# Two bit operations of a weight conversion write to PSUM instead of SBUF, and come behind another piece of a step

## The chip, the cores and the metric

The kernel runs on one core of a Trainium2 chip. The metric is the time of one execution on the device in microseconds (us); the kernel before takes 1632.99 us (median of three runs).

A core has five engines that run side by side, each with its own queue of instructions, worked in order: TensorE (PE in the profile) multiplies matrices and transposes; VectorE (DVE) and ScalarE (ACT) work element by element; GpSimd (POOL) does so too; SyncE (SP) issues the transfers (DMA) from and to device memory. Data lie in SBUF; PE writes its products to PSUM, [...]from which DVE and ACT fetch them. An instruction that needs another engine's result, or a buffer that another engine still reads, waits on a semaphore, and everything behind it in the same queue waits too.

## The reference

Attention with a threshold, a Fourier mix over sequence and model dimension, and a layer-normed channel product with a residual (8 batches, 8 heads, 576 tokens, head size 64, so a model width of 512; the hidden width is 2048):

```python
scores = (1.0 / np.sqrt(64)) * np.matmul(q, k.transpose(0, 1, 3, 2))
thresh = np.max(scores, axis=-1, keepdims=True) - tau
scores = np.where(scores >= thresh, scores, -1e9)
attn = np.exp(scores - np.max(scores, axis=-1, keepdims=True))
attn = attn / (np.sum(attn, axis=-1, keepdims=True) + 1e-09)
x = heads_side_by_side(np.matmul(attn, v))            # (8, 576, 512)

u = x + np.real(np.fft.fft(np.fft.fft(x, axis=1), axis=2))
un = (u - mean(u)) / np.sqrt(var(u) + 1e-06)           # over the 512
out = u + np.maximum(un @ w_ch1, 0.0) @ w_ch2          # 512 -> 2048 -> 512
```

The two weight matrices `w_ch1` and `w_ch2` arrive as 64-bit floats. The engines compute in 32-bit floats, so the kernel converts the weights on the chip, from the bit patterns: this is the part that the change touches.

## The kernel before

**Steps.** The attention is cut into 160 steps: 8 batches, 4 pairs of heads, 5 query tiles. `step(i)` does the 20 steps of the first batch, `second_batch(i)` those of the second, a loop at the end the others. In a step, `scores(i)` multiplies queries by keys on PE (L431, for the last tile L437) into the PSUM tile `sc`; `softmax(i)` takes the row maximum on DVE (L455), the exponential on ACT (L463), and the threshold and the sum on DVE (L471). `transposed_weights(i - 1)` transposes the weights of the step before on PE, in the PSUM tiles `pe` (L534, L537) and `pw` (L552), from which ACT copies them to SBUF (`ends` L540 and L544, `e_t` L554 and L556). `weighted_values` multiplies them by the values on PE (`pv`, L581); DVE or ACT fetches the result (L587, L589).

**Filling.** From the second batch on, PE also has the Fourier mix of the batch before (`mixing`: tiles `py` L684, `pa` L701; POOL folds at L614 and adds at L727) and the channel product of ready tokens (`channels`: `rows.load` transposes to `pn`, L774, which ACT copies at L779 and L780; `hidden` makes `ph`, L814, which ACT (L819) and DVE (L821) read in turn). `fill()` puts some of it into a step, three times a step.

**Order.** Over the first two batches everything is in `manual_schedule`: the order of the instructions on every engine is the order in which the Python code emits them. From the third batch on (L1394) that holds for PE alone, the others being ordered by a scheduler.

**PSUM.** Two double banks have the tag `sc`. The other four banks have the tag `mm`, and all other tiles share them: `pd` (products that fill PE, L112), `pm` (column means, L361), `pr` (mirrored rows, L371), and `pe`, `pw`, `pv`, `py`, `pa`, `pn`, `ph`, `po`. A new tile takes over the bank of an earlier one, and the first instruction that writes to it waits for the last one that read the earlier tile.

**Conversion.** `convert` (L280) is a generator; each `next` emits one stage of one chunk of 128 x 512 weights. There are 32 chunks, 16 of `w_ch1` in the first batch (one for each of the steps 0 to 15) and 16 of `w_ch2` in the second, in the order of `PLAN` (L1268), with two chunks in some steps. The stages:

1. SP's DMA brings 512 KB of raw pairs of 32-bit words (L287) into a stretch of `hs`, or where room is (`w`, `stage`).
2. DVE takes the top 20 bits of the mantissa (L297) to the destination in `w1` or `w2` (`w` in the profile), and the 11 bits of the exponent (L300) to `power`, which lies in `hs` or `u_t`.
3. ACT turns the mantissa into a float from 1 to 2 (L305) and the exponent into the bit pattern of a power of two (L308).
4. DVE adds the low word's part of the mantissa (L312).
5. POOL multiplies by the power (L317).
6. ACT takes the sign (L319), POOL multiplies by it (L320).

In the first batch stages 4 to 6 of a chunk are emitted in the next step's softmax. Then, in the chunk's own step, come

```python
if i in chunks:
    next(chunks[i])            # stage 2
if i > 0:
    transposed_weights(i - 1)
if i in chunks:
    next(chunks[i])            # stage 3
```

In `second_batch` stages 2 and 3 come side by side, by two calls of `advance(first)`, behind `transposed_weights`. Where a step has two chunks, `advance` emits stage 2 of both and then stage 3 of both. After the conversion of four chunks of `w_ch1` that make up 512 columns, PE forms the columns' means, and DVE and POOL subtract them (`less_mean`, L377).

Of the kernel before, what the change touches and what calls it, by code (L numbers as in the profile page):

```python
# [10 lines left out]
INT32 = mybir.dt.int32  # L11
UINT32 = mybir.dt.uint32
ALU = mybir.AluOpType
ACT = mybir.ActivationFunctionType
# [33 lines left out]
def kernel(  # L48
# [25 lines left out]
    WC = 512  # L74
# [10 lines left out]
    ps = ctx.enter_context(tc.tile_pool(name="ps", bufs=2, space=bass.MemoryType.PSUM))  # L85
# [19 lines left out]
    def busy(n):  # L105

        for _ in range(n):
            pd = ps.tile([128, 4, 128], FP32, tag="mm", bufs=4, name="pd")
            four = bass.AP(
                tensor=ones.tensor, offset=ones.offset, ap=[list(ones.ap[0]), [0, 4], [1, 128]]  # L110
            )
            nc.tensor.matmul(pd[:, :, :], ones[:, :], four, start=True, stop=True)  # L112
# [31 lines left out]
    def load_v(n):  # L144

        b, p = n // NPAIR, PAIRS[n % NPAIR]
        vt = v_in[n % 2]
        for j in range(2):
            h = 2 * p + (j + p) % 2
            nc.sync.dma_start(  # L150
                out=vt[:, j:8:2, :], in_=v[b, h, 0:512, :].rearrange("(t p) d -> p t d", p=128)
            )
            nc.sync.dma_start(out=vt[64 * j : 64 * j + 64, 8 + j, :], in_=v[b, h, 512:576, :])
# [12 lines left out]
    for u in range(2):  # L166
# [14 lines left out]
        out=q_scale[:], in0=tau_t[:], scalar1=0.0, scalar2=SCALE, op0=ALU.is_ge, op1=ALU.mult  # L181
# [3 lines left out]
        out=below[:], in0=tau_t[:], scalar1=0.0, scalar2=-3.0e38, op0=ALU.is_lt, op1=ALU.mult  # L185
# [3 lines left out]
        out=tau_pos[:], in0=tau_t[:], scalar1=0.0, scalar2=-1.0, op0=ALU.max, op1=ALU.mult  # L189
# [87 lines left out]
    shift = const.tile([128, 1], FP32, name="shift")  # L277
    nc.vector.memset(shift[:], -float((1023 - 127) << 23))

    def convert(src, dst, raw, power):  # L280

        if src.dtype == FP32:
            nc.sync.dma_start(out=dst, in_=src)
            return
        nc.sync.dma_start(out=raw, in_=src.bitcast(INT32).rearrange("p (c n) -> p c n", c=2))  # L287
        pairs = raw.rearrange("p c (n two) -> p c n two", two=2)
        low, high = pairs[:, :, :, 0], pairs[:, :, :, 1]
        dst = dst.rearrange("p (c n) -> p c n", c=2)  # L290
        bits = dst.bitcast(INT32)
        power = power.rearrange("p (c n) -> p c n", c=2)
        sign = high.bitcast(FP32)

        yield

        nc.vector.tensor_scalar(  # L297
            out=bits, in0=high, scalar1=0xFFFFF, scalar2=None, op0=ALU.bitwise_and
        )
        nc.vector.tensor_scalar(  # L300
            out=power, in0=high, scalar1=20, scalar2=0x7FF,
            op0=ALU.logical_shift_right, op1=ALU.bitwise_and,
        )
        yield
        nc.scalar.activation(out=dst, in_=bits, func=ACT.Copy, bias=1.0, scale=2.0**-20)  # L305


        nc.scalar.activation(  # L308
            out=power, in_=power, func=ACT.Relu, bias=shift[:, :], scale=float(1 << 23)
        )  # L310
        yield
        nc.vector.scalar_tensor_tensor(  # L312
            out=dst, in0=low.bitcast(UINT32), scalar=2.0**-52, in1=dst,
            op0=ALU.mult, op1=ALU.add,
        )
        yield
        nc.gpsimd.tensor_tensor(out=dst, in0=dst, in1=power.bitcast(FP32), op=ALU.mult)  # L317
        yield
        nc.scalar.activation(out=sign, in_=high, func=ACT.Sign)  # L319
        nc.gpsimd.tensor_tensor(out=dst, in0=dst, in1=sign, op=ALU.mult)  # L320
# [100 lines left out]
    def scores(i):  # L421
        n, t = divmod(i, NT)
        qT, kT = heads[n][0:2]

        nh = 2 if t < 4 else 1
        sc = [ps.tile([128, 2, 512], FP32, tag="sc", name=f"sc{j}") for j in range(nh)]
        if t < 4:
            for c in range(2):
                for j in range(2):
                    hp, k0 = slice(64 * j, 64 * j + 64), D * (1 - j)  # L430
                    nc.tensor.matmul(  # L431
                        sc[j][:, c, 0:HALF], qT[hp, 128 * t : 128 * t + 128],
                        kT[hp, k0 + HALF * c : k0 + HALF * (c + 1)], start=True, stop=True,
                    )
        else:
            for c in range(2):
                nc.tensor.matmul(  # L437
                    sc[0][:, c, 0:HALF], q_ends[:, :], kT[:, D + HALF * c : D + HALF * (c + 1)],
                    start=True, stop=True,
                )  # L440
        steps[i] = (sc, nh)
# [735 lines left out]
    def step(i):  # L1177

        n, t = divmod(i, NT)
        scores(i)  # L1180

        def stages(count):
            for _ in range(count if i - 1 in chunks else 0):
                next(chunks[i - 1], None)

        def next_stages():
            stages(2)

        def last_stage():
            stages(1)  # L1190
            chunks.pop(i - 1, None)

        if t == 1 and n > 0:
            softmax(i, lambda: weighted_values(n - 1, 1), next_stages, last_stage)
            load_v(n + 1)
        elif t == 3:
            softmax(i, lambda: weighted_values(n, 0), next_stages, last_stage)
        else:
            softmax(i, None, next_stages, last_stage)
        if t == 1 and n > 0:  # L1200
            pass
        elif later and later[0][0] <= i:
            later.pop(0)[1](i)
        else:
            busy(2 if i < NCHUNK else 1)
        if t == 2:
            scale_q(n + 1)
        if t == 3:
            prep_pair(n + 1)
        if t == 1:  # L1210
            prep_ends(n)
        if i in chunks:
            next(chunks[i])
        if i > 0:
            transposed_weights(i - 1)
        if i in chunks:
            next(chunks[i])
        while after and after[0][0] <= i:
            after.pop(0)[1]()
        if i > 0 and i + 3 < NCHUNK:  # L1220
            chunks[i + 3] = w1_chunk(i + 3)
        if t == 2 and n > 0:
            folds.append(fold_rows(n - 1))
        if folds and next(folds[0], True):
            folds.pop(0)
# [26 lines left out]
    chunks = {0: w1_chunk(0)}  # L1252
# [27 lines left out]
    chunks = {}  # L1280

    def advance(at):
        for run in chunks.get(at, ()):
            next(run, None)

    def transfers(first):
# [32 lines left out]
    def second_batch(i):  # L1319

        nonlocal budget
        n, t = divmod(i, NT)
        first = i - per_batch
        if first != 1:
            scores(i)
        if first == 0:

            transposed_weights(i - 1)
        softmax(
            i, None, lambda: (advance(first - 1), advance(first - 1)), lambda: advance(first - 1)  # L1330
        )
        chunks.pop(first - 1, None)
        transfers(first)
        fold_more()
        if first == 0:
            weighted_values(n - 1, 1)
            scores(i + 1)
            column_means(LAST)
            copy_mean(LAST)
            folds.append(fold_rows(n - 1))  # L1340
            while folds:
                fold_more()
            load_v(n + 1)
            start_batch(0)
            mix(3)
            mix(3)
        elif first == 1:
            mix(3)
            transposed_weights(i - 1)
            mix(2)  # L1350
            mirrored(LAST)
            for c, eng in ((1, nc.vector), (3, nc.vector), (0, nc.gpsimd), (2, nc.gpsimd)):
                less_mean(eng, LAST, c)
            advance(first)
            advance(first)
        elif first == 2:
            mix(2)
            transposed_weights(i - 1)
            mix(2)
            weighted_values(n, 0)  # L1360
            advance(first)
            advance(first)
        else:
            fill()
            transposed_weights(i - 1)
            advance(first)
            advance(first)
            fill()
            if t == 3:
                prep_pair(n + 1)  # L1370
            fill()
            if t == 2:
                weighted_values(n, 0)
            if t == 0:
                weighted_values(n - 1, 1)
                folds.append(fold_rows(n - 1))
                load_v(n + 1)
        if t == 1:
            prep_ends(n)
        if t == 2:  # L1380
            scale_q(n + 1)
        if first == 16:
            fold_halves(1)
        if first < 3:
            budget += 3 * per_slot
# [95 lines left out]
```

## Time and profile before

| | |
|---|---|
| runs | 1632.99, 1632.99, 1630.95 us |
| span of the profiled execution | 1631.3 us |
| busy, share of the span | PE 97%, DVE 72%, ACT 50%, POOL 40% |
| busy, 0 to 115 us | PE 103.17, DVE 101.61, ACT 79.03, POOL 87.31 us |
| busy, 115 to 265 us (150 us) | PE 136.19, DVE 123.00, ACT 93.75, POOL 86.71 us |
| busy, 265 to 1631 us (1366 us) | PE 1344.41, DVE 948.79, ACT 644.99, POOL 485.25 us |

"Busy" is the time in which an engine was executing, in one profiled execution. The chain that ended last is followed back from the last instruction, at each step to what released it; it tells which engine set the time. A row of a tile or a line gives the number of instructions with the least, median and greatest duration in ns. A row of the timeline gives start, duration, engine, line, operation, the tile written and the tiles read, the shapes, the count, and in brackets the idle time before it with what ended it. The granted PE clock is 1.00 at full speed.

### The profile page before, as it was taken

The numbers are of one execution on the slowest core, as the hardware profiler recorded it, in microseconds if no ns is written. First come the engines' busy times: TensorE is split into PE (matmuls) and PEld (weight loads), VectorE is DVE, ScalarE is ACT, GpSimd is POOL, SyncE is SP. The second block draws the span as 40 slices with busy tenths as digits, with TensorE's granted clock in tenths as the row PEclk, the third lists the DMA queues.
The fourth block names the chain that finished last, engine by engine and source line by source line (L and its number), as shares of the span: only waits on it lengthen the run. The fifth ranks groups of instructions, "written<-read, shape, count | busy, mean of one in ns | idle before, by whom it ended". The sixth has DMA issues, their size and how long they took to land.

```text
span 1631.3 us, 27898 instructions
## 1 busy us (share of the span) xinstructions
PE 1583.8 (97%) x10346; PEld 1248.7 (77%) x10346; DVE 1173.4 (72%) x2518; ACT 817.8 (50%) x1738; POOL 659.3 (40%) x875
## 2 busy tenths in 40 slices
PE   8998999999999999999999999999999999999998
PEld 4555655577887888878888778877878788889998
DVE  7997886667758686857576868786787869664445
ACT  5765665544455454645445546454636455523111
POOL 6784673042421452244342244224352344124332
PEclk9999999999999999999999999999999999999999
DMA  6423222101110101110011010111111110000000
GB/s 162 123 56 113 74 75 57 40 17 22 20 38 17 34 9 43 23 29 16 21 23 36 17 34 11 41 23 35 17 27 32 22 29 2 14 7 7 14 14 14
DMA packets 203084, 57.41 MB, mean 35 GB/s; under 512 B 193827, under 2 KB 193829, under 8 KB 202950
## 3 DMA queue, kind: packets, MB, share of 16 engines
q1 hardware_dynamic: 200438, 55.34, 14.5%
q8 instruction: 82, 1.34, 0.4%
q10 hardware_dynamic: 2512, 0.30, 0.1%
q14 instruction: 52, 0.43, 0.1%
HBM read 46.02 MB, written 9.44 MB: 34 GB/s over the span
## 4 chain that ended last, share of the span: by engine, by line
PE 77%; DVE 14%; ACT 4%; POOL 2%; issue 2%; DMA 1%; SPq 1%; DVEq 0%; ACTq 0%; POOLq 0%
PE ph L918 24%; PE po L1082 20%; PE pv L581 9%; PE sc L431 7%; PE pw L552 6%; PE po L840 3%; DVE neg L455 2%; DVE e L471 2%; PE ph L814 2%; PE sc L437 1%; ACT e L463 1%; PE pn L774 1%; PE py L684 1%; PE pa L701 1%; DVE hs L1043 1%
## 5 line engine op out<-in xcount | busy, mean ns | idle before, releaser
L463 ACT ACTIVATE e<-sc,neg 128x576 f32<-128x576 f32 x288 | 212.5, 738 | 224.7 <-DVE neg L455 224.5
L455 DVE TENSOR_REDUCE neg<-sc 128x1 f32<-128x576 f32 x288 | 207.3, 748 | 161.6 <-PE sc L431 149.7
L471 DVE SCALAR_TENSOR_TENSOR e<-sc,thr,e 128x576 f32<-128x576 f32 x288 | 229.4, 812 | 42.2 <-ACT thr L467 40.4
L1082 PE MATMUL po<-w,hs 128*128 128x256 f32 x1024 | 246.2, 383 | 0.0
L1082 PEld LDWEIGHTS po<-w,hs 128*128 128x128 f32 x1024 | 186.1, 190 | 33.8 <-issue 12.8
L918 PE MATMUL ph<-u_t,w 128*128 128x128 f32 x1536 | 188.1, 277 | 0.0
L431 PE MATMUL sc<-kT,qT 64*128 64x288 f32 x1024 | 174.4, 433 | 12.6 <-DVE e L471 11.1
L918 PEld LDWEIGHTS ph<-u_t,w 128*128 128x128 f32 x1536 | 180.2, 193 | 5.0 <-issue 3.7
L552 PE MATMUL pw<-ident,e 128*128 128x128 f32 x1152 | 170.7, 275 | 7.8 <-ACT y_o L689 2.3
L554 ACT COPY e_t<-pw 128x512 f32<-128x512 f32 x256 | 148.8, 594 | 48.9 <-PE pw L552 48.2
L927 DVE TENSOR_TENSOR hs<-ph,hs 128x512 f32<-128x512 f32 x160 | 106.9, 685 | 70.7 <-PE ph L918 54.0
L431 PEld LDWEIGHTS sc<-kT,qT 64*128 64x128 f32 x1024 | 96.0, 187 | 78.1 <-issue 37.5
L552 PEld LDWEIGHTS pw<-ident,e 128*128 128x128 f32 x1152 | 134.9, 141 | 27.2 <-ACT y_o L689 4.2
L918 PE MATMUL ph<-t_u,s_w 128*128 128x128 f32 x1024 | 126.7, 277 | 2.1 <-POOL t_u L892 1.8
L918 PEld LDWEIGHTS ph<-t_u,s_w 128*128 128x128 f32 x1024 | 119.9, 192 | 7.4 <-issue 4.6
L1082 PE MATMUL po<-hs,s_tile 128*128 128x256 f32 x512 | 121.5, 381 | 0.0
L796 DVE SCALAR_TENSOR_TENSOR u<-po,rstd,u 128x256 f32<-128x256 f32 (+1 forms) x164 | 75.3, 483 | 63.9 <-PE po L1082 62.8
L492 ACT ACTIVATE e<-e,den 128x576 f32<-128x576 f32 x96 | 74.6, 777 | 76.5 <-DVE den L485 76.0
L1082 PEld LDWEIGHTS po<-hs,s_tile 128*128 128x128 f32 x512 | 94.0, 190 | 13.7 <-issue 2.5
L935 ACT ACTIVATE hs<-hs 128x512 f32<-128x512 f32 x112 | 69.2, 630 | 61.6 <-DVE hs L927 61.6
L614 POOL TENSOR_TENSOR half<-x 128x287 f32<-128x287 f32 x48 | 40.5, 865 | 119.5 <-ACT x L587 61.1
L1078 POOL TENSOR_TENSOR hs<-hs,s_tile 128x512 f32<-128x512 f32 x32 | 42.0, 1314 | 107.9 <-PE po L1082 85.0
(194 smaller groups left out, 2899.5 us busy)
## 6 DMA issues: line engine op xcount, KB each, us to landing
hs<-in_moe_w_ch_dram SPq DMA_DIRECT2D x23, 512.0 KB, 4.8
q_in<-in_q_dram SPq DMA_DIRECT2D x128, 72.0 KB, 2.5
out_dram<-u SPq DMA_DIRECT2D x36, 256.0 KB, 2.2
k_in<-in_k_dram SPq DMA_DIRECT2D x124, 72.0 KB, 2.5
v_in<-in_v_dram SPq DMA_DIRECT2D x64, 128.0 KB, 2.4
w<-in_moe_w_ch_dram SPq DMA_DIRECT2D x6, 512.0 KB, 3.6
stage<-in_moe_w_ch_dram SPq DMA_DIRECT2D x3, 512.0 KB, 3.6
v_in<-in_v_dram SPq DMA_DIRECT2D x64, 16.0 KB, 2.2
```

What stands on the lines that cost most here:

```text
L431: nc.tensor.matmul(sc[j][:, c, 0:HALF], qT[hp, 128 * t : 128 * t + 128], kT[hp, k0 + HALF * c : k0 + HALF * (c + 1)], start=True, stop=True,)
L455: nc.vector.tensor_reduce(out=neg[:, j : j + 1], in_=sc[j][:, :, 0:HALF], axis=AXIS_XY, op=ALU.max, negate=True,)
L463: nc.scalar.activation(out=ej, in_=sc[j][:, :, 0:HALF], func=ACT.Exp, bias=neg[:, j : j + 1], scale=1.0)
L471: nc.vector.scalar_tensor_tensor(out=ej, in0=sc[j][:, :, 0:HALF], scalar=thr[:, j : j + 1], in1=ej, op0=ALU.is_ge, op1=ALU.mult, accum_out ...
L492: nc.scalar.activation(out=e[:, S : 2 * S], in_=e[:, S : 2 * S], func=ACT.Copy, scale=den[:, 1:2])
L552: nc.tensor.transpose(pw[:, c, :], e[:, c0 : c0 + 128], ident[:, :])
L554: nc.scalar.copy(e_t[:, 4 * j : 4 * j + 4, qs], pw[:, :, :])
L581: nc.tensor.matmul(pv[64 * j : 64 * j + 64, 0:m], vt[:, 2 * c + j, :], e_t[:, 4 * j + c, 0:m] if c < 4 else ends[:, 0, 0:m], start=(c == 0 ...
L796: nc.vector.scalar_tensor_tensor(out=u, in0=product, scalar=self.rstd[:, t : t + 1], in1=u, op0=ALU.mult, op1=ALU.add,)
L918: nc.tensor.matmul(banks[name][:, 128 * q : 128 * q + 128], left[c][:, 512 * part + 128 * q : 512 * part + 128 * q + 128], right[c], start ...
L927: nc.vector.tensor_tensor(out=to, in0=bank, in1=to if other is None else other, op=ALU.add)
L1082: nc.tensor.matmul(bank[:, 0 : DM // 2], left[p], right[p], start=start and p == 0, stop=p == NK - 1, skip_group_check=True,)
```

## The change

The two bit operations of stage 2 write to two new PSUM tiles, `bits` and `exponent`, of the tag `mm`, and ACT's two operations of stage 3 read from there; ACT writes to the same places in SBUF as before. In the first batch, stage 2 is emitted behind `transposed_weights(i - 1)` and directly ahead of stage 3. In the second batch, `first_stages` emits both stages of one chunk before those of the next chunk, where two calls of `advance` emitted stage 2 of both chunks first.

```diff
-        bits = dst.bitcast(INT32)
         power = power.rearrange("p (c n) -> p c n", c=2)
         sign = high.bitcast(FP32)
 
         yield
+        bits, exponent = (
+            ps.tile([128, 2, WC // 2], INT32, tag="mm", bufs=4, name=name)[:, :, :]
+            for name in ("bits", "exponent")
+        )
         nc.vector.tensor_scalar(
             out=bits, in0=high, scalar1=0xFFFFF, scalar2=None, op0=ALU.bitwise_and
         )
         nc.vector.tensor_scalar(
-            out=power, in0=high, scalar1=20, scalar2=0x7FF,
+            out=exponent, in0=high, scalar1=20, scalar2=0x7FF,
             op0=ALU.logical_shift_right, op1=ALU.bitwise_and,
         )
         yield
...
         nc.scalar.activation(
-            out=power, in_=power, func=ACT.Relu, bias=shift[:, :], scale=float(1 << 23)
+            out=power, in_=exponent, func=ACT.Relu, bias=shift[:, :], scale=float(1 << 23)
         )
...
-        if i in chunks:
-            next(chunks[i])
         if i > 0:
             transposed_weights(i - 1)
         if i in chunks:
+            next(chunks[i])
             next(chunks[i])
...
+    def first_stages(at):
+        for run in chunks.get(at, ()):
+            next(run, None)
+            next(run, None)
...                                # in second_batch, at three places
-            advance(first)
-            advance(first)
+            first_stages(first)
```

More of the change, by code (lines that the diff above doesn't have):

```diff
@@ L1360, in second_batch @@
             weighted_values(n, 0)
-            advance(first)
-            advance(first)
+            first_stages(first)
         else:
@@ L1365, in second_batch @@
             transposed_weights(i - 1)
-            advance(first)
-            advance(first)
+            first_stages(first)
             fill()
```

## The prediction

> **What bounds the kernel now.** I read the chain that ended last first, then the 40 slices, then engine busy time by window in the two batches where weights are converted.
>
> ```profile
> PE   8998999999999999999999999999999999999998
> DVE  7997886667758686857576868786787869664445
> ...
> PE 77%; DVE 14%; ACT 4%; POOL 2%; issue 2%; DMA 1%; SPq 1%; DVEq 0%; ACTq 0%; POOLq 0%
> ```
>
> TensorE (PE) carries 77% of the chain and VectorE (DVE) 14%. The conversions lie in the first 255 us, so I split there. Columns: window, its length, busy time of PE, weight load, DVE, ACT, POOL, granted PE clock, DMA share, GB/s.
>
> ```profile
> 15.00:40.00 25.00, 22.17 (x112) 12.87 (x110) 23.86 (x51) 18.57 (x37) 19.20 (x25) 1.00 0.72 176
> 65.00:90.00 25.00, 23.25 (x124) 13.29 (x125) 23.91 (x51) 20.01 (x42) 19.29 (x22) 1.00 0.44 110
> 180.00:210.00 30.00, 25.80 (x136) 16.17 (x132) 26.50 (x55) 20.57 (x46) 19.74 (x26) 1.00 0.29 84
> 265.00:424.00 159.00, 157.92 (x959) 106.94 (x958) 106.61 (x239) 79.55 (x174) 50.91 (x76) 1.00 0.14 28
> ```
>
> In the first batch (to 115 us) DVE sets the pace: 23.9 of 25 us. In the second PE and DVE share it, 25.8 and 26.5 of 30; neither has much slack. From 265 us PE alone does (157.92 of 159.00), so a delay that stands at 255 us stays to the end. Now the changed operations themselves: minimum, median and maximum in ns, then the pair on the chain.
>
> ```profile
> L297 DVE TENSOR_SCALAR w<-hs x23: 384/739/1504, 14.9 to 229.3; 128x512 int32<-128x512 int32 x23
> L300 DVE TENSOR_SCALAR hs<-hs x23: 418/536/1522, 15.3 to 230.3; 128x512 int32<-128x512 int32 x23
> L312 DVE SCALAR_TENSOR_TENSOR w<-hs,w x23: 673/678/1664, 17.1 to 232.1; 128x512 f32<-128x512 uint32 x23
> ...
> 38.01 1.29 POOL L320 TENSOR_TENSOR w<-w,hs 128x512 f32<-128x512 f32 x1
> 38.16 1.42 DVE L297 TENSOR_SCALAR w<-hs 128x512 int32<-128x512 int32 x1
> ```
>
> The same instruction takes 0.38 or 1.5 us. The long ones lie beside a POOL instruction: L297 starts 0.15 us after POOL's L320 and ends just after it.
>
> [...]no bit operation of this trace writes to PSUM, so the price after is unseen.[...]
>
> **The change part by part.** On PE and SP the order of instructions is identical, on DVE and ACT too apart from the 64 outputs and 64 inputs renamed; POOL moves two small copies (L523, L529) past each other's neighbours, at no cost, as POOL is at 20 of 30 us. No DMA moves. Three things remain.
>
> *1. DVE's price.* The pair L297 + L300 totals 55.4 us over 32 chunks (25.9 + 29.5, all forms).[...] The price is between 0.38 each[...] and 0.68 (L312, same size[...]); I take the upper, 0.60 from start to start, so 1.27 a pair. The 16 pairs of batch 1 occupy 25.3 us and would occupy 20.3: 4.9 less. Only where DVE ends the wait does it count: going along the chain from 10 to 120 us, eleven chunks have a piece of L297/L300 in it (14.97 us), and 1.27 in place of each leaves a net gain of 3.7 us; between 43.7 and 56.7 us PE holds the chain and hides the rest. At 0.38 each it would be about 8. In batch 2 DVE gets some of this back too (counted inside 3).
>
> *2. POOL and ACT.* POOL is no longer held by these DVE instructions. Its chain from 149 to 161 us has L727 at 0.99 to 1.21 where 0.65 is the free time, and L723 at 0.87 for 0.68: 0.9 us gained. ACT reads 512 elements from PSUM in 594 ns (L554), from SBUF in 633 (L305): nothing, ACT being 50% busy.
>
> *3. Banks.* All of PE's small products (pd, pe, pw, pv, pm, pr, pa, py, pn, ph, po) take turns in the four banks tagged "mm". A new tile takes the bank given back longest ago and waits for its last reader. Two more tiles a chunk turn this ring, so that PE's tiles wait for other readers. I followed the ring through both programs, in the order in which their instructions stand. In batch 1 PE has slack behind DVE: I find one wait of 1.2 us (pd of the tenth chunk on ACT's L305), hidden there, and 0.3 elsewhere. In batch 2 the tiles of the channel product (ph, L814) stood behind tiles that were long free; now they stand behind pw, whose reader L554 sits late in ACT's queue:
>
> ```profile
> 170.29 2.75 PE L814 MATMUL ph<-u_t,w 128*128 128x384 f32 x8
> 172.42 1.08 ACT L554 COPY e_t<-pw 128x512 f32<-128x512 f32 x2
> 172.96 1.24 PE L431 MATMUL sc<-kT,qT 64*128 64x288 f32 x8
> 174.92 0.60 PE L774 MATMUL pn<-ident,u_t 128*128 128x128 f32 x4
> 178.22 1.11 DVE L297 TENSOR_SCALAR w<-w 128x512 int32<-128x512 int32 x1
> 179.37 0.63 ACT L305 ACTIVATE w<-w 128x512 f32<-128x512 int32 x1 [1.07 <-DVE w L297]
> 181.19 1.24 PE L431 MATMUL sc<-kT,qT 64*128 64x288 f32 x8
> ```
>
> Here ph must wait from 170.29 to the end of L554 at about 173.0: 2.8 us. Behind it in PE's queue are the scores (L431), for which DVE (L455) and ACT (L463) wait; so it is on the path. Next pn waits for L305 of the same step, the "bits" being read at 179.4 to 180.0 (ph and pv behind it wait likewise): up to the scores at 181.19 the delay sums to 7.4, of which DVE has 5.8. The same reading further on:
>
> ```profile
> 226.34 2.75 PE L814 MATMUL ph<-u_t,w 128*128 128x384 f32 x8
> 228.42 1.08 ACT L554 COPY e_t<-pw 128x512 f32<-128x512 f32 x2
> ...
> 232.09 2.85 PE L814 MATMUL ph<-u_t,w 128*128 128x384 f32 x8 [0.30 <-ACT hs L819]
> 234.19 1.09 ACT L554 COPY e_t<-pw 128x512 f32<-128x512 f32 x2
> ...
> 245.12 2.85 PE L814 MATMUL ph<-u_t,w 128*128 128x384 f32 x8
> 249.66 1.08 ACT L554 COPY e_t<-pw 128x512 f32<-128x512 f32 x2
> ```
>
> At 184.33 ph waits in the same way for L554 at 187.77: the delay at DVE rises to 7.3, at 195 (pv on DVE's L821) to 7.9. The steps at 203.7 and 211.7, with two chunks each, give back DVE time (4.35 us of bit operations become 2.4 a step): 5.6. Then 218.5 (a tile behind L544) 7.4; 226.34 to 229.0 adds 2.7, 9.7 to 10; 232.09 to 234.8 adds 2.7 less what DVE hides, 12.3; 245.12 to 250.2 is 5.1, of which 3.4 arrives, DVE being slack by 1.7: **15.7** at 255 us.
>
> *The clock.* Gaps on PE are followed by half clock already in this trace:
>
> ```profile
> 210.00:212.00 2.00, 0.96 (x4) 0.87 (x5) 1.93 (x7) 2.00 (x6) 2.00 (x2) 0.59 0.79 128
> 212.00:214.00 2.00, 2.00 (x5) 0.83 (x3) 2.00 (x2) 1.05 (x2) 2.00 (x3) 0.50 0.80 132
> ```
>
> After 1.92 us idle at 209 to 211, eight ph matmuls take 4.79 us where they take 2.75 elsewhere. The stretches at 102, 162 and 210 us cost 1.7, 1.7 and about 3.4 us of PE work. Six waits of part 3 are over 2 us; I take four of them to cost 2 on the path each: +8, bounds 0 and 14.
>
> Sum: −3.7 − 0.9 + 15.7 + 8 = +19 on the span of 1631.3, so 1650.4. The runs lie at 1630.95 to 1632.99, with the profiled span 1.7 below the median: **1652 us**.
>
> **Rivals.** A difference of 0.2% (3.3 us) is about what a measurement of this kernel can tell from no change.
> A (0.52), as above: waits and half clock, 1652; own range 1645 to 1662.
> B (0.28), waits without the clock: [...]DVE hides the slow stretches. +11, 1644; range 1637 to 1648. For it: the slow stretch at 213 us was mostly hidden. Against: each gap above is longer than the 1.9 us that sufficed.
> C (0.14), faster: PE's new waits are hidden in batch 2 as in batch 1, because DVE and ACT come earlier[...], and L554 with them. Only the gain of 3.7 to 4.9 shows: 1628.5. For it: 32 pairs at 1.73 on average become 1.27, 7 us in batch 2 alone. Against: ph needs L554 2.7 us earlier, and one pair gives 0.5. It decides if the waits that reach DVE in batch 2 sum to less than 4.6 us, the gain of parts 1 and 2.
> D (0.06), writes to PSUM dearer than 0.68, or chained waits that I did not follow: 1662 and more.
> The change cannot fail to do what it says: every L297 and L300 has its output renamed.
>
> **Numbers.** The range 1634 to 1664 holds A, B and a little of D, and leaves out C and the rest of D, 0.19. Slower: A, B and D less 0.02 for a B that shrinks to the bound, 0.84; same: these 0.02 and 0.02 of C, 0.04; faster 0.12.
>
> **What would show it.** Price: L297 and L300 with a maximum near their minimum, between 0.4 and 0.7 us, and POOL's L320 unstretched. Path: batch 1 ends about 4 us earlier. Banks: PE idle of 2 to 5 us ahead of L814 and L774 from 170 us, ended by ACT e_t L554 and ACT w L305, and some 20 us lost by 265 us; after that equal windows. Clock: granted clock below 0.8 in four or more further windows. Wrong if PE's idle ahead of L814 in batch 2 is small, if scores do not wait behind it, or if the bit operations get longer than 0.8 us.

## The result, and the profile after

The changed kernel takes 1653.08 us (median of four runs, 1650.31 to 1655.18) where the kernel before takes 1632.59. The ratio is 1.0126, with a 95% interval of 1.0109 to 1.0144: 18 to 24 us slower. The forecast was 1652 us. The profiled execution of the kernel after is the fastest of its four, with 1650.31 us.

Lines from L297 to L312 of the kernel before stand 4 further down in the one after (the bit operations are L301 and L304, their readers on ACT L309 and L312), as do the later ones that are named here: L814 is L818, the `e_t` copy L554 is L558. In the other kernels below the lines shown stand up to 13 further down than before; the tiles' names say which line is meant.

The slices and the shares of the chain that ended last, of the kernel after:

```profile
PE   8998788999999999999999999999999999999998
DVE  7988575667767677866676758787787868664445
...
PE 78%; DVE 13%; ACT 5%; issue 2%; POOL 1%; DMA 0%; DVEq 0%; ACTq 0%; POOLq 0%
```

Each slice is 41 us. The fifth to seventh of PE (165 to 288 us) are 7, 8 and 8; the others look as before. The chain has 5% of ACT where it had 4, so PE waits for ACT somewhere. The windows say where: same columns as in the prediction.

```profile
65.00:90.00 25.00, 23.91 (x131) 13.56 (x130) 23.98 (x55) 20.39 (x41) 18.40 (x20) 1.00 0.48 128
115.00:165.00 50.00, 45.19 (x264) 28.83 (x264) 40.12 (x95) 26.71 (x59) 27.25 (x38) 1.00 0.29 92
165.00:283.00 118.00, 92.83 (x439) 55.07 (x438) 74.83 (x170) 65.79 (x136) 54.19 (x70) 0.91 0.26 65
283.00:442.00 159.00, 157.92 (x956) 106.71 (x955) 106.61 (x240) 79.35 (x174) 50.65 (x74) 1.00 0.14 27
```

and the kernel before, over the stretch that answers to the third line:

```profile
165.00:265.00 100.00, 92.33 (x452) 55.95 (x451) 82.49 (x174) 67.41 (x141) 59.51 (x71) 0.96 0.30 75
```

PE is busy for about the same 92 to 93 us, but spreads it over 118 us in place of 100, at a mean clock of 0.91 in place of 0.96. From 283 us on everything is as it was from 265 on, so what was lost stays lost.

The new waits of PE from 120 to 290 us, after (microseconds in total, times, the longest):

```profile
PE ph L818 <- ACT e_t L558: 16.2, 6, 5.1
PE pn L778 <- ACT w L309: 4.6, 1, 4.6
PE ph L818 <- ACT w L309: 1.7, 2, 0.9
```

and all that `ph` waited for before, from 120 to 270 us:

```profile
PE ph L814 <- POOL u_t L727: 2.0, 1, 2.0
...
PE ph L814 <- ACT hs L819: 0.3, 1, 0.3
```

One by one, in PE's timeline of the kernel after (the bracket has the wait and its releaser):

```profile
169.30 2.85 PE L818 MATMUL ph<-u_t,w 128*128 128x384 f32 x8 [2.61 <-ACT e_t L558]
178.69 1.11 PE L778 MATMUL pn<-ident,u_t 128*128 128x128 f32 x4 [4.57 <-ACT w L309]
191.95 4.54 PE L818 MATMUL ph<-u_t,w 128*128 128x384 f32 x8 [3.10 <-ACT e_t L558]
235.85 4.54 PE L818 MATMUL ph<-u_t,w 128*128 128x384 f32 x8 [2.54 <-ACT e_t L558]
245.32 2.85 PE L818 MATMUL ph<-u_t,w 128*128 128x384 f32 x8 [2.52 <-ACT e_t L558]
263.08 5.00 PE L818 MATMUL ph<-u_t,w 128*128 128x384 f32 x8 [5.09 <-ACT e_t L558]
```

These are the six places that the prediction named. In three of them the eight products themselves take 4.5 to 5.0 us where the others take 2.85: PE works at half clock behind the wait. The granted clock is 0.62, 0.62 and 0.56 over the eight products at 191.95, 235.85 and 263.08 us (0.50 from 192.4 to 194.4, from 237 to 239 and from 263.08 to 266 us), and 1.00 over those at 169.30 and 245.32. Why `e_t` is late is seen in the chain of the kernel after ahead of the third of them:

```profile
190.05 1.11 ACT w L323 x2
191.16 0.26 ACT ends L544
191.41 0.50 ACT e_t L558
...
191.95 4.54 PE ph L818 x8
```

PE had written `pw` by 188.9 us; ACT gets to it behind two signs (stage 6) and the copy of `ends`. ACT's order is the same before; only then no `ph` stood behind this copy.

The bit operations, after (minimum, median, maximum in ns):

```profile
L301 DVE TENSOR_SCALAR bits<-hs x23: 665/684/698, 15.6 to 236.1; 128x512 int32<-128x512 int32 x23
L304 DVE TENSOR_SCALAR exponent<-hs x23: 669/684/695, 16.2 to 236.7; 128x512 int32<-128x512 int32 x23
L316 DVE SCALAR_TENSOR_TENSOR w<-hs,w x23: 678/682/1946, 18.1 to 242.9; 128x512 f32<-128x512 uint32 x23
```

The spread of 0.38 to 1.5 us is gone; each takes 0.68. POOL's products by the sign (L320, up to 1.59 us before) take 1.31 us at most.

### The profile page after: what moved, and what is told of

Same layout as the page of the kernel before. It is cut to its first block, busy times and chain, and to the rows that moved or that the text cites. A ratio compares the mean times of both kernels' runs of the same rounds, so it can differ in the third digit from the quotient of the medians.

```text
span 1648.3 us, 27935 instructions
## 1 busy us (share of the span) xinstructions
PE 1585.5 (96%) x10346; PEld 1247.8 (76%) x10346; DVE 1164.2 (71%) x2518; ACT 816.9 (50%) x1738; POOL 648.7 (39%) x875
## 4 chain that ended last, share of the span: by engine, by line
PE 78%; DVE 13%; ACT 5%; issue 2%; POOL 1%; DMA 0%; DVEq 0%; ACTq 0%; POOLq 0%
PE ph L922 23%; PE po L1086 20%; PE pv L585 9%; PE sc L435 8%; PE pw L556 5%; PE ph L818 3%; PE po L844 3%; DVE neg L459 3%; DVE e L475 2%; ACT e L467 2%; PE sc L441 1%; PE pn L778 1%; PE py L688 1%; PE pa L705 1%; DVE hs L1047 1%
## 5 line engine op out<-in xcount | busy, mean ns | idle before, releaser
L435 PE MATMUL sc<-kT,qT 64*128 64x288 f32 x1024 | 170.8, 431 | 7.7 <-DVE e L475 5.7
L558 ACT COPY e_t<-pw 128x512 f32<-128x512 f32 x256 | 148.6, 593 | 48.5 <-PE pw L556 47.9
L818 PE MATMUL ph<-u_t,w 128*128 128x384 f32 (+1 forms) x256 | 69.5, 424 | 19.2 <-ACT e_t L558 16.2
```

Source lines behind the costliest of these rows:

```text
L435: nc.tensor.matmul(sc[j][:, c, 0:HALF], qT[hp, 128 * t : 128 * t + 128], kT[hp, k0 + HALF * c : k0 + HALF * (c + 1)], start=True, stop=True,)
L558: nc.scalar.copy(e_t[:, 4 * j : 4 * j + 4, qs], pw[:, :, :])
L818: nc.tensor.matmul(ph[:, a:z], w1[c][:, 128 * j : 128 * (j + 1)], u_t[:, c, at : at + z - a], start=(c == 0), stop=(c == ND - 1), skip_gro ...
```

## The experiments

All are timed beside the kernel before on the same chip; its medians there were 1633.01, 1633.28 and 1632.64 us. Theory: PE's waits for banks in batch 2, and the half clock behind them. Main rival: the price of the operations that write or read PSUM.

**Which batch.** The condition around the new tiles, for the first weights or for the second:

```diff
+        if src.tensor.name == w_ch1.tensor.name:      # second run: w_ch2
+            bits, exponent = (
...
+        else:
+            bits, exponent = dst.bitcast(INT32), power
```

> bits and exponent go to PSUM for the 16 chunks of the first weights only (batch 1); the second weights' chunks write to SBUF as before. Theory of the banks (the loss is PE waiting in batch 2 for banks whose readers come late): no wait of over 1 us ahead of ph L814 in batch 2, 1629 to 1632 us, which is the gain of batch 1 alone. Rival, price (the loss is the dearer bit operations and what reads them, 32 chunks alike): half of the loss stays, 1640 to 1645 us.

Measured: 1630.84 us, ratio 0.9986 (0.9979 to 0.9993): faster than before.

> The other half: PSUM for the 16 chunks of the second weights only (batch 2). Theory of the banks: the whole loss, and a little more since batch 1's gain is gone, 1653 to 1657 us, with the same waits of 2.5 to 5 us ahead of L814 and L774. Rival, price: half of the loss, 1640 to 1645 us.

Measured: 1653.78 us, ratio 1.0132 (1.0113 to 1.0152), with 16.2, 4.6 and 1.7 us of waits in the same three lines. The whole loss is in batch 2, although both batches convert 16 chunks with the same operations.

**The ring without the price.** The bit operations write to SBUF, two tiles with one element each take the banks:

```diff
+        bits, exponent = dst.bitcast(INT32), power
+        small = []
+        if src.tensor.name == w_ch2.tensor.name:
+            small = [ps.tile([128, 512], FP32, tag="mm", bufs=4, name=name) for name in ("bits", "exponent")]
...
+            nc.vector.memset(tile_[0:1, 0:1], 0.0)             # behind each bit operation
...
+            nc.scalar.copy(seen[0:1, 0:1], tile_[0:1, 0:1])    # behind L305 and behind L308
```

> The bit operations write to SBUF as before in both batches (so 0.38 to 1.5 us each, VectorE and GpSimd holding each other up as before), in the changed program's order. In batch 2 two small tiles of the tag mm take the places of bits and exponent: DVE writes one element to each right by its bit operation, ACT reads it right behind L305 and L308. Theory of the banks: PE waits ahead of L814 behind e_t L554 as in the changed kernel (2.6, 3.1, 2.5, 2.5, 5.1 us) and some 4.6 ahead of pn L774; 1650 to 1658 us though no bit operation touches PSUM. Rival, price: the small operations alone, 1633 to 1636 us.

Measured: 1661.83 us, ratio 1.0177 (1.0160 to 1.0193). PE's waits from 160 to 290 us in this run (`seen` is written by ACT's small copies):

```profile
PE ph L827 <- ACT e_t L567: 15.8, 5, 5.1
PE pn L787 <- ACT seen L316: 5.1, 1, 5.1
PE ph L827 <- ACT ends L557: 3.3, 1, 3.3
PE ph L827 <- ACT seen L316: 2.0, 2, 1.4
```

The waits come without any bit operation in PSUM, so they come from the ring. The kernel is slower than the changed one and than the 1658 expected at most. Likely reasons are that the long bit operations (L302 and L307, 0.87 and 0.81 us in the mean from `hs`) and the small copies stand ahead of what PE now waits for, and that none of the cheaper price is there to pay back; also, the granted clock over batch 2's conversions is lower (0.87 from 157 to 290 us, where the run with PSUM in batch 2 has 0.91 from 157 to 283). No run separates these.

**The order alone.** The changed order of emission, with `bits, exponent = dst.bitcast(INT32), power` for all chunks:

> The changed program's order of emission, with bits and exponent in SBUF as before in both batches: nothing takes a bank. All theories but one expect no change, 1632 to 1634 us, since the order on PE, DVE and ACT is the same; if the order itself cost something, up to 1636.

Measured: 1632.16 us, ratio 0.9999 (0.9990 to 1.0008). The order costs nothing and gives nothing.

**One tile instead of two.**

```diff
-        bits, exponent = (
...
+        bits = ps.tile([128, 2, WC // 2], INT32, tag="mm", bufs=4, name="bits")[:, :, :]
+        exponent = power
```

> Only bits goes to PSUM, exponent to SBUF as before: one tile a chunk in the ring where the change has two. Followed through the ring, ph then stands behind ends L540, which ACT does directly ahead of e_t L554, so its waits are shorter by 0.5 to 0.6 us only, about 2.2, 2.8, 3.0, 2.0, 2.0 and 4.6. Theory of the banks: most of the loss with one tile, 1645 to 1651 us. Rival, a loss that grows with the number of tiles or of PSUM writes: half, about 1642.

Measured: 1644.83 us, ratio 1.0080 (1.0065 to 1.0095), a little below the range given for the theory and above the rival's 1642. PE's waits from 160 to 290 us:

```profile
PE ph L816 <- ACT ends L542: 13.5, 5, 4.6
PE pn L776 <- ACT ends L546: 2.6, 1, 2.6
```

The waits have the sizes worked out, to within 0.4 us, and the releaser `ends` that the ring gives, ACT's instruction just ahead of `e_t`. Time alone would not have told the two theories apart; the releaser does.

**One wait.** Of the 32 chunks only the one of the fifteenth step of batch 2 has its tiles in PSUM (`held[0] = at == 14` in `first_stages`, and SBUF where it is false).

> SBUF for all chunks but the one of the fifteenth step of batch 2, which alone has bits and exponent in PSUM. Ahead of the fourteenth ph one wait of 5.1 us on e_t L554 should stand, and no other new one over 0.7. Theory of waits plus clock: 3.4 us of it arrive and 1.7 to 3.4 us of half clock come on top, 1637 to 1640 us. Rival, no cost of the clock: +3 to +3.6, 1636. Rival, price: 1633.

Measured: 1637.55 us, ratio 1.0031 (1.0020 to 1.0043), and in PE's timeline

```profile
250.28 4.80 PE L823 MATMUL ph<-u_t,w 128*128 128x384 f32 x8 [4.79 <-ACT e_t L563]
```

One wait of 4.8 us, with the products behind it at half clock (4.80 us for the eight; granted clock 0.62 from 249 to 256 us). The scores' maximum (L455) is taken 288 times in every kernel here, in the same order, so the start of the n-th can be compared between traces. The 64th starts 5.6 us later than before, where the 61st was still in step: wait and slow clock together, within the 5.1 to 6.8 worked out. By the medians it is 4.3 us (3.3 to 7.0 by the interval, which does not shut out the 3.6 of the rival without a cost of the clock; the trace speaks against it): 1.2 us of the difference between the traces goes at about 730 us, where the trace before has a half-clock stretch (0.50 from 730 to 732 us) that this one has not. A second new wait in batch 2 was not expected, 1.75 us ahead of `pv` at 221 us; L455 stays in step behind it.

**The clock.** PE is given work for the time in which it would wait: six `pw` tiles are transposed several times over.

```diff
-            for c in range(4):
+            pws[0] += 1
+            for c in [0, 1, 2, 3] * (1 + {44: 4, 45: 5, 47: 5, 56: 4, 58: 4, 62: 8}.get(pws[0], 0)):
                 c0 = (S + D) * j + 128 * c
                 nc.tensor.transpose(pw[:, c, :], e[:, c0 : c0 + 128], ident[:, :])
```

> The changed kernel with PE kept at work while it would stand still: six pw tiles of batch 2 (those ahead of the third, fifth, eleventh, twelfth and fourteenth ph and the first pn) are transposed 4 to 8 times more, the same values to the same place; their readers on ACT come later than that anyway, so ph still starts when L554 has read its bank. If the half clock behind each wait costs time (my +8): most of the half-clock stretches from 165 to 270 us go, and 4 to 9 us with them, 1644 to 1649 us beside 1653. Rival (the slow stretches lie in slack, the waits alone are the loss): within 2 us of the changed kernel, or slower where a repetition runs past its wait.

> The changed kernel itself, on the same chip as the others: 1650 to 1656 us.

Measured: 1648.87 us filled, 1651.95 for the changed kernel beside it; ratios to before 1.0102 (1.0084 to 1.0120) and 1.0116 (1.0100 to 1.0132). The same step, first in the changed kernel, then filled (the wait of 0.97 is what the repetition left over):

```profile
191.50:196.50 5.00, 4.55 (x10) 2.31 (x10) 1.92 (x6) 2.17 (x4) 5.00 (x6) 0.66 0.57 140
```

```profile
192.00:197.00 5.00, 4.29 (x17) 2.42 (x18) 2.37 (x7) 2.92 (x6) 5.00 (x7) 1.00 0.50 128
...
192.71 2.85 PE L821 MATMUL ph<-u_t,w 128*128 128x384 f32 x8 [0.97 <-ACT e_t L561]
```

The clock stays at 1.00 and `ph` takes 2.85 us again. Over all of batch 2's conversions the granted clock rises from 0.90 (control, 157 to 280 us) to 0.99 (filled, 157 to 273), and the delay at the 67th L455 is 13.5 us against before in place of 20.0. So the half clock costs up to 6.5 us there; 4.1 of them are left at the end of the two traces and 3.1 in the medians. Part of the difference between these three numbers is a half-clock stretch near 740 us, which this trace has and the control's has not. What decides about that stretch was not tried. The intervals of the two ratios overlap, so the 3.1 alone would not settle it. The clock column and the start of the 67th L455 do so for these two executions, one of each kernel.

**A better place.** Both stages go to the end of the step, behind the last fill, where `ph` has its bank already:

```diff
             fill()
             transposed_weights(i - 1)
-            first_stages(first)
             fill()
...
                 load_v(n + 1)
+            first_stages(first)
```

> As the changed kernel, but from the third step of batch 2 on both stages of a chunk come at the end of the step, behind the last fill and the weighted values, so that ph takes its bank before bits and exponent do. Theory of the banks: the waits behind L554 vanish, waits of up to 1.3 us remain (pw, ph on L305 and L819); half clock stretches as in the kernel before; 1626 to 1636 us. Rival, price: as the changed kernel, about 1653 us.

Measured: 1627.50 us, ratio 0.9970 (0.9961 to 0.9979), faster than both kernels. The waits behind `e_t` ahead of `ph` are gone; one behind L305 is left, longer than the 1.3 us allowed for:

```profile
PE ph L818 <- ACT w L309: 2.7, 1, 2.7
```

Taking that away too, with SBUF in the steps that have two chunks:

> A version meant to be better than both: stages at the end of the step as in late_stages, and in the three steps of batch 2 with two chunks the bit operations write to SBUF as before, which takes away the wait of 2.7 us ahead of ph at 203 us that late_stages still had. Theory of banks: 1624 to 1627 us, 1 to 3 below late_stages (1627.5); against: the two-chunk steps lose the cheaper pairs (4.35 us of bit operations where 2.7 would be), so it may come out equal, 1627 to 1630.

Measured: 1628.05 us, ratio 0.9967 (0.9957 to 0.9978). The wait is gone from the trace, and the time is the same. The expectation of 1624 to 1627 was missed. That the dearer pairs in three steps cost what the wait had cost is argued, not shown; it fits that PE now waits 3.5 us in all for DVE's `e` ahead of the scores from 120 to 290 us, where it waited 1.0.

> late_stages with the second weights' bit operations in SBUF (the first weights' in PSUM): tells where the 3 us come from by which late_stages (1627.5) lies below the run with PSUM in batch 1 alone (1630.8). If they come from PSUM's cheaper pairs in batch 2: 1630 to 1633 us; if from the later place of the stages: 1627 to 1628.

Measured: 1628.71 us, ratio 0.9975 (0.9968 to 0.9982). These runs were not all made on one chip, so the ratios are compared. From PSUM in batch 1 alone (0.9986) to the late place with SBUF in batch 2 (0.9975) it is 1.8 us, from there to the late place with PSUM (0.9970) another 0.8. In both steps the intervals overlap. So the later place probably gives the larger part, but these runs do not show it, and what PSUM adds in batch 2 cannot be told from nothing. Why the later place should help was not looked into.

## Why the prediction was right, and where its sizes were off

**Banks.** Right in place and cause, and in the sizes of the waits. Those forecast ahead of `ph` and `pn` were 2.8, about 4.6 (7.4 less 2.8), 2.7, 2.7 and 5.1; the trace has 2.61, 4.57, 2.54, 2.52 and 5.09, and 3.10 at the third place, for which the prediction gave only its endpoints. One more, 1.8 us at 218.5 us behind L544, is 0.3 in the kernel after and 1.8 in the filled run. The sum of 15.7 that was to arrive at DVE is best compared with the filled run, where the clock is nearly out of it: its 67th L455 is 13.5 us late, having been 1.6 early at 157 us, so 15.1 us arrived. This agrees better than the comparison allows, for the kernel before has half-clock stretches of its own from 157 us on that the filled run has not (granted clock 0.95 from 157 to 260 us, against 0.99); the waits alone have cost somewhat more than 15.1. That the ring makes them is shown by the run of the ring without the price, beside that of the order without the ring (1.0177 and 0.9999).

**The clock.** Right in kind, too large in size: 8 was taken (0 to 14), and 3.1 to 6.5 were measured between the changed kernel and the filled one. What comes on top of the kernel before, for which the 8 stood, is less. From the windows above (length times what the clock lacks of 1.00), half clock takes about 12 us of PE's time in the control run, 1 in the filled run and 5 in the kernel before. If the same share of it arrives, the excess over before is some 4 us, an estimate. The sign given came out, just: four stretches at half clock behind the new waits (from 178.7, 192.4, 236.7 and 260.6 us, the granted clock of the first 2 us or so of each being 0.50 or 0.51).

Not every wait over 2 us brought a half-clock stretch. In the profile shown above the first (2.61) and the fifth (2.52) had none behind them, while the control run's first had one: the same wait of 2.61 us was followed by 2.85 us for the eight products in one execution and by 4.54 in the other. What decides between the two was not shown.

**VectorE's price.** The choice of 0.68 for each operation was exact (0.684). That POOL would hold up none of them was an assumption; none of the 64 takes over 0.70 us in the trace after. The gain in batch 1 was not: 3.7 forecast, 2.2 measured in the run with PSUM in batch 1 alone (1633.01 to 1630.84; interval of the ratio 0.7 to 2.1 per mille, so 1.1 to 3.4 us). The sign of about 4 us at the end of batch 1 did not appear either: the 34th L455 (117 us) starts 2.0 us early in that run's trace and 1.3 in the trace after.

The step that failed is "1.27 in place of each leaves a net gain of 3.7", for two reasons. The first is its sum. Eleven chunks at 1.27 are 13.97 us, which leaves 1.0 of the 14.97. With 0.60 for the three chunks of which L297 alone lies on the chain it is 3.0. It comes to 3.7 only if the six chunks that gain are added up and those that get dearer are left out, such as this one, 0.75 us on the chain before:

```profile
80.37 0.32 DVE w L297
80.69 0.43 DVE hs L300
```

The second is that it took all hold-ups by POOL as gone with the two operations. One moved on to another DVE instruction that reads SBUF. First the kernel before, then the one after:

```profile
101.61 0.68 DVE L312 SCALAR_TENSOR_TENSOR w<-hs,w 128x512 f32<-128x512 uint32 x1
...
101.70 1.92 POOL L643 TENSOR_TENSOR sums<-f 128x608 f32<-128x608 f32 x1
```

```profile
99.73 1.47 POOL L647 TENSOR_TENSOR sums<-f 128x608 f32<-128x608 f32 x1
99.81 1.95 DVE L316 SCALAR_TENSOR_TENSOR w<-hs,w 128x512 f32<-128x512 uint32 x1
```

Before, DVE came first by 0.09 us and POOL was held (1.92 instead of 1.47); after, POOL came first by 0.08 and DVE was held: 1.27 us more than its 0.68, on the chain. All seven traces of kernels with both bit operations of batch 1 in PSUM show this hold (1.95 to 2.00 us), the traces of the other six kernels do not. In the trace with PSUM in batch 1 alone, DVE is 2.3 us ahead of the kernel before at the L455 just in front of it and 1.2 at the L471 just behind it. No run takes the hold away, so how much of the missing 1.5 us it explains is not shown.

**POOL.** 0.9 us forecast on its chain at 149 to 161 us; the wait of `ph` for POOL's `u_t` was 1.96 us before and is 0.95 after. What the forecast had not counted: behind this wait the kernel before has a half-clock stretch (from 162.6 us, granted clock 0.50 up to 166.0) that is absent after (1.00 from 115 to 165 us).

**The sum.** −3.7 − 0.9 + 15.7 + 8 was +19. In the traces, at the 67th L455, it is −1.6 up to 157 us and +15.1 from there on with the clock kept up (POOL's gain is inside it), so 13.5 in the filled run; half clock adds 6.5, so 20.0 in the control run. Of these, 18.4 are left at the end of the trace; 1.2 us go at about 730 us, where only the trace before has a half-clock stretch. By the medians the changed kernel is 18.7 slower in that comparison and 20.5 in the first. The 1.8 between the two comparisons are not explained. That 1652 lies within 1.1 us of both medians of the changed kernel (1653.08 and 1651.95) is in part luck: batch 1 gave 1.5 us less than forecast and the clock cost at least 1.5 less, and these two misses cancel.

**The rivals.** C (faster, waits hidden) was decided by its own criterion: it needed less than 4.6 us of waits that reach DVE, and 15.1 arrived. Its gain alone is what the run with PSUM in batch 1 shows. B (waits without a cost of the clock, 1644) lies 8 us below the control run, and the 6.5 us between the traces of control and filled run speak against it; part of the half clock is hidden, as B said, for 6.5 of some 11 us arrive. B's 1644 is also 5 us below the filled run's 1648.87, in which the repetitions leave a half-clock stretch behind `pn` and some waits. D is out: the operations take 0.68 us, and from 120 to 290 us PE has no new wait of over 1 us but the six.

## What to carry to other kernels

A tile in a shared pool of banks can cost more than its own write and read: it shifts which earlier reader every later tile waits for (16.2 us of waits ahead of `ph` here, and 1.0177 with no bit operation in PSUM). Before adding one, follow the pool through the written order and ask of each tile ahead of a busy engine who frees its bank and when; a bank freed by an instruction deep in another engine's queue is a wait even if the data were ready long ago (3.10 us ahead of `ph` at 191.95 us, for a `pw` written by 188.9). If the new tile can be emitted behind the tile that must not wait, the loss (1.0126) can go: here it turned into a gain (0.9970), of which PSUM in batch 1 alone gives about half (0.9986).

## What the runs showed of the hardware

L312, a DVE instruction with two SBUF inputs (0.68 us for 512 elements when free), was held up beside POOL, though its shortest time is 0.67 us and not the 0.38 of the bit operations in SBUF: it took 1.95 us in the kernel after and 2.00 in the run with PSUM in batch 1 alone, where POOL had started 0.08 and 0.04 us earlier. The 64 bit operations that write 128x512 to PSUM were not held once (0.665 to 0.698 us), although 57 of them run beside a POOL instruction in the trace. And PE's clock was kept up here by work that was not useful: repeated transposes in a gap kept it at 1.00 where it fell to 0.66 without them, over 5 us each. Waits of under a microsecond were followed by half clock too: in the kernel after, PE waits 0.95 and 0.83 us between 216.7 and 219.7 us, and a stretch at half clock begins at 219.7 (granted clock 0.50 up to 222.0).
